# Cosine attention followed by a two-layer GELU network, fused: head pairs on 128 partitions, x kept on chip, second matmul between the next batch's attention steps

## The chip, the cores and the metric

One core of one Trainium2 chip. The metric is the device time of one execution in microseconds (us); below, "span" is the time from the first to the last instruction in the trace, which for the kernel before is 21 us shorter than the measured time. PE is the engine for matmuls; DVE, ACT and POOL are the vector, scalar and GpSimd engines; SP issues transfers. Every figure is of fast runs (within 1.5% of the kernel's fastest).

## The reference, cut to what matters

```python
# q, k, v: (8, 12, 448, 64) float32, tau = 0.1
q_n = q / (norm(q) + 1e-6);  k_n = k / (norm(k) + 1e-6)
attn = softmax(q_n @ k_n.T / tau) @ v                 # per batch and head
x = attn.transpose(0, 2, 1, 3).reshape(8 * 448, 768)  # tokens x d_model
h = x @ w_in                                          # 768 -> 2048
out = gelu_exact(h) @ w_out                           # 2048 -> 768
```

## The kernel before

All 96 heads come first, one by one; then the two matrix products, in blocks of 512 tokens. `x` goes through a bf16 tensor in device memory between the halves.

```python
for b in range(B):
    for h in range(H):
        # ... DMA q, k, v; v to bf16 on POOL with a column of ones ...
        nc.scalar.activation(sq, qk, AF.Square)
        nc.vector.tensor_reduce(nq, sq, mybir.AxisListType.X, ALU.add)
        nc.vector.reciprocal(rn, nq)
        nc.scalar.sqrt(inq, rn)                       # another table than exp
        nc.gpsimd.tensor_tensor(qkb, qk, inq.to_broadcast([CS, NT, 2, D]), ALU.mult)
        # ... 4 transposes on PE, 2 copies on DVE ...
        for c in range(NT):
            nc.tensor.matmul(st, lhsT=qknT[:, 1, c, :], rhs=qknT[:, 0, :, :], start=True, stop=True)
            nc.scalar.activation(pt, st, AF.Exp, scale=float(inv_tau))
            nc.tensor.matmul(acc, lhsT=v1[:, c, :], rhs=pt, start=(c == 0), stop=(c == NT - 1))
        nc.vector.reciprocal(rec, acc[D:D + 1, :])    # 448 values on one partition
        nc.gpsimd.partition_broadcast(rb_, rec)
        nc.vector.tensor_tensor(oT, acc[0:D, :], rb_, ALU.mult)
        nc.sync.dma_start(out=xT[h * D:(h + 1) * D, b * S:(b + 1) * S], in_=oT)
# ... weights loaded and cast on DVE ...
for rb in range(NRB):                                 # 7 blocks of 512 tokens
    # ... load x; first product and gelu; second product, copy, store ...
```

Of the kernel before, what the change touches and what calls it, by code (L numbers as in the profile page):

```python
# [8 lines left out]
F32 = mybir.dt.float32  # L9
BF16 = mybir.dt.bfloat16  # L10
AF = mybir.ActivationFunctionType
ALU = mybir.AluOpType


@with_exitstack
def kernel(
    ctx: ExitStack,
    tc: tile.TileContext,
    q: bass.AP,
    k: bass.AP,  # L20
    v: bass.AP,
    tau: float,
    moe_w_in: bass.AP,
    moe_w_out: bass.AP,
    out: bass.AP,
):
    nc = tc.nc
    B, H, S, D = q.shape
    NT = 4
    CS = S // NT  # L30
    d_model = H * D
    n_tok = B * S
    d_ff = moe_w_in.shape[1]
    inv_tau = 1.0 / float(tau)

    xT = nc.dram_tensor("xT_bridge", (d_model, n_tok), BF16, kind="Internal").ap()

    consts = ctx.enter_context(tc.tile_pool(name="consts", bufs=1))
    ident = consts.tile([CS, CS], BF16)
    make_identity(nc, ident)  # L40

    qkp = ctx.enter_context(tc.tile_pool(name="qkp", bufs=3))
    vp = ctx.enter_context(tc.tile_pool(name="vp", bufs=2))
    hdp = ctx.enter_context(tc.tile_pool(name="hdp", bufs=2))
    stp = ctx.enter_context(tc.tile_pool(name="stp", bufs=3))
    attn_ps = ExitStack()
    ps = attn_ps.enter_context(tc.tile_pool(name="ps", bufs=2, space=bass.MemoryType.PSUM))
    ps2 = attn_ps.enter_context(tc.tile_pool(name="ps2", bufs=3, space=bass.MemoryType.PSUM))

    for b in range(B):  # L50
        for h in range(H):
            qk = qkp.tile([CS, NT, 2, D], F32, tag="qk")
            nc.sync.dma_start(out=qk[:, :, 0, :],
                              in_=q[b, h].rearrange("(c p) d -> p c d", c=NT))
            nc.sync.dma_start(out=qk[:, :, 1, :],
                              in_=k[b, h].rearrange("(c p) d -> p c d", c=NT))
            vf = qkp.tile([CS, NT, D], F32, tag="vf")
            nc.sync.dma_start(out=vf, in_=v[b, h].rearrange("(c p) d -> p c d", c=NT))
            v1 = vp.tile([CS, NT, D + 1], BF16, tag="v1")
            nc.vector.memset(v1[:, :, D], 1.0)  # L60
            nc.gpsimd.tensor_copy(v1[:, :, :D], vf)  # L61

            sq = qkp.tile([CS, NT, 2, D], F32, tag="sq")
            nc.scalar.activation(sq, qk, AF.Square)  # L64
            nq = qkp.tile([CS, NT, 2], F32, tag="nq")
            nc.vector.tensor_reduce(nq, sq, mybir.AxisListType.X, ALU.add)  # L66
            rn = qkp.tile([CS, NT, 2], F32, tag="rn")
            nc.vector.reciprocal(rn, nq)  # L68
            inq = qkp.tile([CS, NT, 2], F32, tag="inq")
            nc.scalar.sqrt(inq, rn)  # L70
            qkb = qkp.tile([CS, NT, 2, D], BF16, tag="qkb")
            nc.gpsimd.tensor_tensor(qkb, qk,  # L72
                                    inq.to_broadcast([CS, NT, 2, D]), ALU.mult)

            tp = ps.tile([2 * D, NT, CS], BF16, tag="tp")
            for c in range(NT):
                nc.tensor.transpose(tp[:, c, :], qkb[:, c, :, :], ident)  # L77
            qknT = hdp.tile([D, 2, NT, CS], BF16, tag="qknT")
            nc.vector.tensor_copy(qknT[:, 0, :, :], tp[0:D, :, :])  # L79
            nc.vector.tensor_copy(qknT[:, 1, :, :], tp[D:2 * D, :, :])  # L80

            acc = ps2.tile([D + 1, S], F32, tag="acc")
            for c in range(NT):
                st = ps2.tile([CS, S], F32, tag="st")
                nc.tensor.matmul(st, lhsT=qknT[:, 1, c, :],  # L85
                                 rhs=qknT[:, 0, :, :], start=True, stop=True)
                pt = stp.tile([CS, S], BF16, tag="pt")
                nc.scalar.activation(pt, st, AF.Exp, scale=float(inv_tau))  # L88
                nc.tensor.matmul(acc, lhsT=v1[:, c, :], rhs=pt,  # L89
                                 start=(c == 0), stop=(c == NT - 1))  # L90
            rec = stp.tile([1, S], F32, tag="rec")
            nc.vector.reciprocal(rec, acc[D:D + 1, :])  # L92
            rb_ = stp.tile([D, S], F32, tag="rb")
            nc.gpsimd.partition_broadcast(rb_, rec)
            oT = stp.tile([D, S], BF16, tag="oT")
            nc.vector.tensor_tensor(oT, acc[0:D, :], rb_, ALU.mult)  # L96
            nc.sync.dma_start(out=xT[h * D:(h + 1) * D, b * S:(b + 1) * S], in_=oT)

    attn_ps.close()

    KD = d_model // 128
    KF = d_ff // 128
    RB = 512
    NRB = n_tok // RB

    wpool = ctx.enter_context(tc.tile_pool(name="wpool", bufs=1))
    wtmp = ctx.enter_context(tc.tile_pool(name="wtmp", bufs=2))
    wi = wpool.tile([128, KD, d_ff], BF16)
    wo = wpool.tile([128, KF, d_model], BF16)
    for kd in range(KD):  # L110
        t = wtmp.tile([128, d_ff], F32, tag="wt1")
        nc.sync.dma_start(out=t, in_=moe_w_in[kd * 128:(kd + 1) * 128, :])
        nc.vector.tensor_copy(wi[:, kd, :], t)
    for kf in range(KF):
        t = wtmp.tile([128, d_model], F32, tag="wt2")
        nc.sync.dma_start(out=t, in_=moe_w_out[kf * 128:(kf + 1) * 128, :])
        nc.vector.tensor_copy(wo[:, kf, :], t)

    xpool = ctx.enter_context(tc.tile_pool(name="xpool", bufs=2))
    gpool = ctx.enter_context(tc.tile_pool(name="gpool", bufs=2))  # L120
    opool = ctx.enter_context(tc.tile_pool(name="opool", bufs=3))
    psm = ctx.enter_context(tc.tile_pool(name="psm", bufs=4, space=bass.MemoryType.PSUM))
    pso = ctx.enter_context(tc.tile_pool(name="pso", bufs=4, space=bass.MemoryType.PSUM))

    NSPLIT = 2
    NSZ = [512, 256]
    NOFF = [0, 512]

    for rb in range(NRB):
        r0 = rb * RB  # L130
        xTb = xpool.tile([128, KD, RB], BF16, tag="xTb")
        for kd in range(KD):
            nc.sync.dma_start(out=xTb[:, kd, :], in_=xT[kd * 128:(kd + 1) * 128, r0:r0 + RB])
        gT = gpool.tile([128, KF, RB], BF16, tag="gT")
        for m in range(KF):
            hp = psm.tile([128, RB], F32, tag="hp")
            for kd in range(KD):
                nc.tensor.matmul(hp, lhsT=wi[:, kd, m * 128:(m + 1) * 128],  # L138
                                 rhs=xTb[:, kd, :],
                                 start=(kd == 0), stop=(kd == KD - 1))  # L140
            nc.scalar.activation(gT[:, m, :], hp, AF.Gelu)  # L141
        for rs in range(RB // 128):
            for ni in range(NSPLIT):
                nsz = NSZ[ni]
                op = pso.tile([128, 512], F32, tag="op")
                for kf in range(KF):
                    nc.tensor.matmul(op[:, :nsz],  # L147
                                     lhsT=gT[:, kf, rs * 128:(rs + 1) * 128],
                                     rhs=wo[:, kf, NOFF[ni]:NOFF[ni] + nsz],
                                     start=(kf == 0), stop=(kf == KF - 1))  # L150
                ot = opool.tile([128, 512], F32, tag="ot")
                nc.vector.tensor_copy(ot[:, :nsz], op[:, :nsz])  # L152
                nc.sync.dma_start(
                    out=out[r0 + rs * 128:r0 + (rs + 1) * 128, NOFF[ni]:NOFF[ni] + nsz],
                    in_=ot[:, :nsz])


# [1 line left out]
_INS = ['q', 'k', 'v', 'tau', 'moe_w_in', 'moe_w_out']  # L159
_OUTS = [((3584, 768), 'float32')]  # L160
#: Inputs that are plain numbers.
_NUMBERS = {'tau': 0.10000000149011612}


# [26 lines left out]
```

## Time and profile before

| | before |
|---|---|
| time, median | 1788 us |
| span of the profiled run | 1767 us |
| attention (96 heads) | 0 to 1471 us |
| two matrix products | 1471 to 1767 us |

The prediction below shows the slices, the chain, the stretches and one head of this profile. Two rows of the page's groups are added here (line, engine, operation, output and input with sizes, count | busy us, mean ns | idle time of the engine before them and what ended it):

```profile
L92 DVE RECIPROCAL rec<-acc 1x448 f32<-1x448 f32 x96 | 283.3, 2952 | 463.2 <-PE acc L89 463.2
L88 ACT ACT_TABLE_LOAD x93 | 119.3, 1283 | 472.1 <-PE st L85 472.1
```

They are to be read together: the reciprocal is DVE's largest item, and DVE stood idle for 463 us before it. An engine that is both busy and waiting like this is a link of a serial chain.

### The profile page before, as it was taken

How to read it: one execution, taken by the hardware profiler on the slowest of the kernel's cores; microseconds unless marked ns; L12 is line 12 of the kernel's file. 1: busy time of each engine (PE TensorE's matmuls, PEld its weight loads, DVE VectorE, ACT ScalarE, POOL GpSimd, SP SyncE). 2: the span in 40 equal slices, each digit the busy share in tenths (PEclk: the TensorE clock that was granted, in tenths of full speed). 3: DMA queues.
4: the chain of work that ended last, by engine and by line, in shares of the span. 5: the costliest groups of instructions: out<-in, count | busy, mean ns of one | idle time of the engine just before them, and what ended most of it. 6: DMA issues, size and time to landing. Idle time of an engine off the chain costs nothing.

```text
span 1767.2 us, 9510 instructions
## 1 busy us (share of the span) xinstructions
PE 700.8 (40%) x2692; PEld 292.8 (17%) x2720; DVE 540.4 (31%) x750; ACT 566.1 (32%) x876; POOL 205.7 (12%) x294
## 2 busy tenths in 40 slices
PE   3222222222222222222222222222222227999999
PEld 1000000000000000000000000000000003555554
DVE  5533332333332333332333333323333331111111
ACT  4333333333333333333333333333333322222222
POOL 1111111111111111111111111111111110000000
PEclk9999999999999999999999999999999999999999
DMA  6511111111111111111111011111111100111111
GB/s 206 164 23 27 27 32 28 34 30 29 30 29 31 28 25 25 27 27 25 27 28 28 22 28 27 26 26 27 28 25 25 27 9 30 57 61 58 60 41 41
DMA packets 158645, 68.27 MB, mean 39 GB/s; under 512 B 137088, under 2 KB 152192, under 8 KB 157824
## 3 DMA queue, kind: packets, MB, share of 16 engines
q1 hardware_dynamic: 158592, 67.67, 14.5%
q8 instruction: 21, 0.34, 0.1%
q14 instruction: 32, 0.26, 0.0%
HBM read 51.12 MB, written 16.52 MB: 38 GB/s over the span
## 4 chain that ended last, share of the span: by engine, by line
PE 39%; issue 29%; DVE 13%; ACT 9%; POOL 6%; DMA 3%; ACTq 0%; POOLq 0%; SPq 0%
PE st L85 10%; PE acc L89 10%; PE hp L138 8%; PE op L147 8%; POOL qkb L72 5%; ACT L70 5%; DVE oT L96 3%; PE tp L77 3%; ACT pt L88 3%; DVE nq L66 3%; DVE qknT L80 2%; DVE qknT L79 2%; DVE rec L92 2%; DMA xTb<-xT_bridge 1%; DMA xT_bridge<-oT 1%
## 5 line engine op out<-in xcount | busy, mean ns | idle before, releaser
L92 DVE RECIPROCAL rec<-acc 1x448 f32<-1x448 f32 x96 | 283.3, 2952 | 463.2 <-PE acc L89 463.2
L77 PE MATMUL tp<-ident,qkb 112*128 112x112 bf16 x384 | 53.2, 294 | 856.8 <-POOL qkb L72 856.8
L88 ACT ACT_TABLE_LOAD x93 | 119.3, 1283 | 472.1 <-PE st L85 472.1
L70 ACT ACT_TABLE_LOAD x93 | 119.3, 1283 | 420.8 <-DVE rn L68 420.7
L85 PE MATMUL st<-qknT 64*112 64x448 bf16 x384 | 190.7, 597 | 85.8 <-DVE qknT L80 84.5
L89 PE MATMUL acc<-pt,v 112*65 112x448 bf16 x384 | 179.3, 565 | 114.5 <-ACT pt L88 114.5
L88 ACT ACTIVATE pt<-st 112x448 bf16<-112x448 f32 x384 | 188.0, 543 | 65.4 <-PE st L85 64.4
L77 PEld LDWEIGHTS <-qkb 112*128 112x128 bf16 x384 | 30.5, 130 | 929.6 <-POOL qkb L72 929.6
L79 DVE COPY qknT<-tp 64x448 bf16<-64x448 bf16 x96 | 36.7, 383 | 469.5 <-PE tp L77 469.5
L72 POOL TENSOR_TENSOR qkb<-qk,inq 112x512 bf16<-112x512 f32 x96 | 99.5, 1037 | 661.5 <-issue 559.5
L138 PE MATMUL hp<-xTb,wi 128*128 128x512 bf16 x658 | 147.5, 383 | 5.5 <-DVE oT L96 4.6
L147 PE MATMUL op<-wo,gT 128*128 128x512 bf16 (+1 forms) x882 | 146.0, 325 | 0.7
L141 ACT ACTIVATE gT<-hp 128x512 bf16<-128x512 f32 x112 | 66.9, 597 | 201.9 <-PE hp L138 201.9
L152 DVE COPY ot<-op 128x512 f32<-128x512 f32 (+1 forms) x56 | 31.3, 558 | 262.3 <-PE op L147 262.3
L85 PEld LDWEIGHTS <-qknT 64*112 64x112 bf16 x384 | 60.9, 187 | 277.1 <-issue 168.4
L147 PEld LDWEIGHTS <-gT 128*128 128x128 bf16 x896 | 87.7, 98 | 59.4
L138 PEld LDWEIGHTS <-wi 128*128 128x128 bf16 x672 | 66.2, 99 | 85.2 <-DVE oT L96 5.8
L89 PEld LDWEIGHTS <-v 112*65 112x65 bf16 x384 | 47.6, 149 | 119.7 <-issue 119.7
L66 DVE TENSOR_REDUCE nq<-sq 112x8 f32<-112x512 f32 x96 | 64.3, 670 | 4.7 <-ACT sq L64 4.7
L64 ACT ACTIVATE sq<-qk 112x512 f32<-112x512 f32 x96 | 59.6, 622 | 0.3 <-DMA qk<-in_k_dram 0.2
L61 POOL CAST v<-vf 112x256 bf16<-112x256 f32 x96 | 48.2, 504 | 5.7 <-issue 5.7
L80 DVE COPY qknT<-tp 64x448 bf16<-64x448 bf16 x96 | 37.7, 393 | 1.3
(205 smaller groups left out, 195.0 us busy)
## 6 DMA issues: line engine op xcount, KB each, us to landing
qk<-in_q_dram SPq DMA_DIRECT2D x96, 112.0 KB, 2.2
qk<-in_k_dram SPq DMA_DIRECT2D x96, 112.0 KB, 2.5
vf<-in_v_dram SPq DMA_DIRECT2D x96, 112.0 KB, 2.1
out_dram<-ot SPq DMA_DIRECT2D x28, 256.0 KB, 2.0
t<-in_moe_w_in_dram SPq DMA_DIRECT2D x6, 1024.0 KB, 5.6
t<-in_moe_w_out_dram SPq DMA_DIRECT2D x16, 384.0 KB, 3.7
xT_bridge<-oT SPq DMA_DIRECT2D x96, 56.0 KB, 1.9
xTb<-xT_bridge SPq DMA_DIRECT2D x42, 128.0 KB, 2.3
```

Source lines behind the costliest of these rows:

```text
L66: nc.vector.tensor_reduce(nq, sq, mybir.AxisListType.X, ALU.add)
L70: nc.scalar.sqrt(inq, rn)
L72: nc.gpsimd.tensor_tensor(qkb, qk, inq.to_broadcast([CS, NT, 2, D]), ALU.mult)
L77: nc.tensor.transpose(tp[:, c, :], qkb[:, c, :, :], ident)
L79: nc.vector.tensor_copy(qknT[:, 0, :, :], tp[0:D, :, :])
L80: nc.vector.tensor_copy(qknT[:, 1, :, :], tp[D:2 * D, :, :])
L85: nc.tensor.matmul(st, lhsT=qknT[:, 1, c, :], rhs=qknT[:, 0, :, :], start=True, stop=True)
L88: nc.scalar.activation(pt, st, AF.Exp, scale=float(inv_tau))
L89: nc.tensor.matmul(acc, lhsT=v1[:, c, :], rhs=pt, start=(c == 0), stop=(c == NT - 1))
L92: nc.vector.reciprocal(rec, acc[D:D + 1, :])
L138: nc.tensor.matmul(hp, lhsT=wi[:, kd, m * 128:(m + 1) * 128], rhs=xTb[:, kd, :], start=(kd == 0), stop=(kd == KD - 1))
L147: nc.tensor.matmul(op[:, :nsz], lhsT=gT[:, kf, rs * 128:(rs + 1) * 128], rhs=wo[:, kf, NOFF[ni]:NOFF[ni] + nsz], start=(kf == 0), stop=(kf ...
```

## The change

The intent: work on two heads at a time, so that 128 partitions are used; lay the score and value matmuls out so that the two heads occupy different halves of PE's array; replace the one-partition reciprocal by ACT's exp(-ln(sum)) on 128 partitions, with the sums made by a matmul against ones; make the norms without ACT's square root (a power on POOL); keep `x` on chip; prepare pairs ahead in a fixed program order; and run the second product of a batch in small pieces ("fillers") between the attention steps of the next batch. Each engine is given its instructions in the order of emission. The diff, cut to its core:

```diff
+    def prep_square(g):                                   # pair g
+        nc.gpsimd.tensor_tensor(sq, qk_t[g], qk_t[g], ALU.mult)
+        nc.vector.tensor_reduce(nq, sq, mybir.AxisListType.X, ALU.add)
+    def prep_scale(g):
+        nc.gpsimd.tensor_tensor(sr, nq, half, ALU.pow)
+        nc.vector.tensor_scalar(se, sr, 1e-6, None, ALU.add)
+        nc.vector.reciprocal(rn, se)
+        # two nc.gpsimd.tensor_tensor(qkb, t, rn, ALU.mult)
+    def transposes(g):
+        # 8 nc.tensor.transpose into one bank, then
+        nc.vector.tensor_copy(qkT, tp)
+    def scores(g, c):                                     # two heads: rows 0:64 and 64:128
+        for h in range(2):
+            nc.tensor.matmul(st[:, h, :S], lhsT=qkT[rows, 1, c, :], rhs=qkT[rows, 0, :, :], ...)
+        nc.scalar.activation(pt, st[:, :, :S], AF.Exp, scale=inv_tau)
+    def values(g, part):                                  # part 0: v, part 1: ones
+        for c in range(NC):
+            for h in range(2):
+                nc.tensor.matmul(dst[h * D:(h + 1) * D, :S], ...)
+    def normalise(g):
+        nc.scalar.activation(ln, sm[:, :S], AF.Ln)
+        nc.scalar.activation(rs, ln, AF.Exp, scale=-1.0)
+        nc.vector.tensor_tensor(x_t[b][:, p, :], o[:, :S], rs, ALU.mult)
...
+        for i in range(HP):                               # attention(b, fill)
+                scores(g, 0); run(u)
+                scores(g, 1); run(u)
+                values(g - 1, 0)
+                scores(g, 2); run(u)
+                values(g - 1, 1)
+                scores(g, 3)
+                normalise(g - 1)
+                upkeep(g)          # loads, prep_square(g + 4), prep_scale(g + 3)
+                run(u)
+                transposes(g + 1)
+                run(...)
...
+    for n in range(1, 4):
+        upto("sq", n, prep_square)
+        upto("sc", n - 1, prep_scale)
+    for kd in range(KD): load_wi(kd)
+    for i in range(4): load_wo(i)
+    upto("sc", 3, prep_scale)
+    transposes(0)
...
+        for m in range(KF):        # first product and gelu of batch b
+            ...
+            if m == KF - 3 and b + 1 < B:
+                transposes((b + 1) * HP)
+        fill += second_pieces(sb, t)
```

## The prediction

> **What bounds the kernel now.** I read four views of the profile, in this order: the page's slices, the chain of work that ended last, the table of stretches, and the timeline of a single head. The slices come first, because they show that the program has two halves that never meet.
>
> ```profile
> PE   3222222222222222222222222222222227999999
> PEld 1000000000000000000000000000000003555554
> DVE  5533332333332333332333333323333331111111
> ACT  4333333333333333333333333333333322222222
> ...
> PE 39%; issue 29%; DVE 13%; ACT 9%; POOL 6%; DMA 3%; ACTq 0%; POOLq 0%; SPq 0%
> ```
>
> For 33 of 40 slices (the attention of 96 heads) no engine is half busy. For the last seven (the two matrix products) PE is full. The last line, the chain by engine, says the same: no engine owns the path, and the time passes from hand to hand. The table of stretches (start:end, length, then busy time and count for PE, weight loads, DVE, ACT, POOL) sets the sizes:
>
> ```profile
> 100.00:700.00 600.00, 166.06 (x468) 56.46 (x468) 197.89 (x269) 203.25 (x310) 82.68 (x117) 1.00 0.12 29
> 1480.00:1767.00 287.00, 282.71 (x1511) 150.28 (x1536) 31.26 (x56) 64.51 (x108) 0.00 (x0) 1.00 0.16 53
> ```
>
> Attention ends at 1471 us, so a head costs 1471 / 96 = 15.3 us; the products take 296 us. One head in the timeline (start, duration, engine, line, operation; in brackets the idle time before it and who ended it):
>
> ```profile
> 698.70 2.95 DVE L92 RECIPROCAL rec<-acc 1x448 f32<-1x448 f32 x1 [5.02 <-PE acc L89]
> 701.69 0.62 DVE L96 TENSOR_TENSOR oT<-acc,rb__2506 64x448 bf16<-64x448 f32 x1
> 702.24 0.67 DVE L66 TENSOR_REDUCE nq<-sq 112x8 f32<-112x512 f32 x1
> 703.22 1.28 ACT L70 ACT_TABLE_LOAD   x1 [4.66 <-DVE rn L68]
> 704.52 0.21 ACT L70 ACTIVATE inq<-rn 112x8 f32<-112x8 f32 x1
> 706.62 1.03 POOL L72 TENSOR_TENSOR qkb<-qk,inq 112x512 bf16<-112x512 f32 x1 [7.09 <-issue]
> 707.71 0.55 PE L77 MATMUL tp<-ident,qkb 112*128 112x112 bf16 x4 [9.05 <-POOL qkb L72]
> 709.15 1.36 PE L85 MATMUL st<-qknT 64*112 64x448 bf16 x3 [0.88 <-DVE qknT L80]
> 709.84 1.28 ACT L88 ACT_TABLE_LOAD   x1 [5.12 <-PE st L85]
> 711.14 1.41 ACT L88 ACTIVATE pt<-st 112x448 bf16<-112x448 f32 x3
> 714.11 2.95 DVE L92 RECIPROCAL rec<-acc 1x448 f32<-1x448 f32 x1 [5.02 <-PE acc L89]
> ```
>
> The reader is to see one long chain per head, with nearly no overlap with the next head: a reciprocal on one partition (2.95), the normalising multiply, the norms of the *next* head queued behind it, a table load for the square root, the square root, the scaling on POOL, transposes, copies, scores, a second table load for the exponential, then the values; 15.4 us after the first reciprocal the next one starts. The kernel is bound by dependence and order, not by an engine.
>
> The same row shows that PE is also slow here: three score matmuls of 448 columns last 1.36 us in all with 0.6 for one, so they start 0.38 apart, 1.2 columns per ns. In the products, at full flow:
>
> ```profile
> 1475.70 18.01 PEld L138 LDWEIGHTS <-wi 128*128 128x128 bf16 x84 [0.22 <-issue]
> ```
>
> 84 steps in 18.01 us are 0.214 us per 512 columns, 2.4 columns per ns. The granted clock reads 1.00 in both stretches and does not show this.
>
> [...]
>
> **The change part by part.**
>
> Removed: the one-partition reciprocal (96 x 2.95 = 283 us, all on the chain), the broadcast on POOL, both table loads per head (186 x 1.283 = 239 us), the square on ACT, the bridge through memory, and the float-to-bf16 copies of v and weights. The order is now fixed so that preparation runs some four pairs ahead; the 15.3 us chain should leave the path altogether, and the question is which engine takes its place. I add each engine for one *pair* of heads (48 of them).
>
> ACT: an exponential of 448 columns takes 543 ns and the gelu of 512 columns 597, so 54 / 64 = 0.84 ns a column and 165 ns fixed. Four exponentials of 896 columns: 4 x 0.92 = 3.7; logarithm and its exponential 2 x 0.54 = 1.1. Sum 4.8 us. In all 48 x 4.8 + 128 gelus x 0.54 + 16 loads x 1.28 = 320 us.
>
> DVE: reduce over 1024 (2 x 0.67 = 1.3), two small operations (0.3), one copy of 896 bf16 columns (0.75), one multiply (0.62): 3.0; with 56 output copies of 0.56 about 175 us. Not the bound.
>
> POOL: scaling of 512 columns takes 1.04, so square of 1024 about 2.05, scaling 2 x 1.04 = 2.1, [...] a wait of about 0.6 for DVE between power and scaling, and the power on 16 columns, for which I leave 1.0 without evidence. Sum 6.7 us.
>
> PE, warm, at 0.42 ns a column: 448 columns 0.188, 384 columns 0.161. Per pair 8 score matmuls = 1.50 and 16 value and sum matmuls = 3.0, both laid out for two tiles of the array at a time. [...] Eight transposes at 0.085 (four take 0.55 with 0.294 for the last): 0.7. The mode changes ten times in a pair (filler, scores, filler, scores, filler, values, scores, filler, sums, scores, transposes). [...] Sum 4.8 us. Filler of 12 or 18 matmuls in a pair adds 1.9 or 2.9: 6.7 or 7.7 us, above ACT's 4.8 and at or above POOL's 6.7. So PE becomes the bound.
>
> The whole span on PE, in us:
> - Batch 0 up to the end of its attention: paced by POOL, which issues six v and ten weight transfers among the first pairs. [...] square and next pair 5.8; [...] third pair 3.7; three pairs at 6.7; last pair through 5: about 60. The 6.3 MB of the first weight, asked for at 21 us, arrive at 0.17 MB/us (the second slice of the page moved 164 GB/s) near 58.
> - First product: 768 x 0.188 = 144.
> - Second product: 896 x 0.161 = 144, all but the last 128 matmuls between attention steps.
> - Attention of seven batches: 42 x 4.8 = 202.
> - Turns of the two shared accumulator banks: where a transpose takes the other bank while an output is summed, the next output wants the bank just filled and waits for its copy, 0.56 (between 425 for 256 columns and 692 for 512) plus a hand-over, 0.65. I count four in a batch of 96 fillers and five in one of 128: 7 x 4.5 x 0.65 = 20. One more for the transposes inside the first product: 7 x 0.9 = 6.
> - Batch starts: exponential table and first exponential before the third score can go, 7 x 2 = 14; end of batch 0, 2.
> - Last copy and store: 3.
>
> Sum 60 + 144 + 144 + 202 + 26 + 16 + 3 = 595. Time exceeds span by 1788.2 - 1767.2 = 21. That gives 616; I say 620.
>
> **The rivals.**
> 1. *Packed matmuls do not overlap.* Then 42 x (4.51 - 2.82) = 71 is added: about 690. For it: the loads of 112 and 65 columns already read 187 and 149 ns each, close to the 188 of a warm matmul, and may not hide when two run together. [...]
> 2. *POOL becomes the bound.* A power of 4 us makes its pair 9.7 against PE's 7.2 on average; and DVE, which executes in order, stands behind the wait for POOL, so copies and then PE stop too: 42 x 2.5 = 105 and 10 in batch 0, about 730. For it: nothing in the trace bounds that operation. Against: it is 16 columns.
> 3. *Perfect packing and free mode changes.* A pair costs 2.26 + 0.7 = 3.0: 42 x 1.8 = 76 less, about 540; with 12 fillers PE would come to 4.9 and share the bound with ACT.
> 4. *ACT reloads tables* between logarithm and exponential: 2.6 more, 7.4 us a pair, at PE's level; perhaps 25 more. Against: both in one set, loaded by hand.
> 5. *The chain survives.* If the next batch still waited for a serial chain, gains would halve, near 1000. Against: four pairs of lead in the order.
>
> **Range and chances.** The middle is the sum. The lower end, 550, is rival 3 with some waits left; the upper, 700, is rival 1 with a little of 2. Even rival 5 leaves the kernel much faster: faster 0.985, same 0.01, slower 0.005.
>
> **What would show it.** In the new profile: PE at nine tenths from about slice 5 on; score matmuls of two heads starting a few ns apart (packing) or 0.19 apart (rival 1); about 16 or 17 table loads; POOL under 400 us busy and its power near 1 us; [...] about 60 us before the first gelu. The prediction is wrong if PE idles more than a fifth of the span after 60 us, if POOL's busy share is near 90%, or if the chain that ended last names DVE or POOL for more than a quarter.

The sum came to 595 us of span (60 + 144 + 144 + 202 + 26 + 16 + 3) and 616 of time; it said 620. The marked cuts took out what no trace or run of this case shows. Terms that are cut, or that have lost their reason, are still in these sums: 1.0 us on POOL for the issue of one transfer (in its 6.7 us a pair, and in batch 0, where 60 was 15 to the first scaled pair, 6 of it for six v transfers, then 5.8, 10 for ten weight transfers, 3.7, three times 6.7, and 5); packed matmuls at 1.6 times the speed (0.94 + 1.88 in place of 1.50 + 3.0); and 0.13 us for each of ten mode changes, that is, changes of the array's division between matmuls (1.3). PE's pair was 0.94 + 1.88 + 0.7 + 1.3 = 4.8. The kernel after shows 0.74 us for the issue of a v transfer, and 0.56 and 0.75 for those of the two weights. The wait of 0.6 us on POOL was my estimate (the kernel after shows 0.57 in its first pairs). That logarithm and exponential share a table was not shown by the kernel before; the kernel after ran its 48 pairs with 16 table loads.

## The result, and the profile after

| | before | after |
|---|---|---|
| time, median | 1788.9 us | 740.5 us (735.9 to 745.5) |
| span of the profiled run | 1767 us | 734.4 us |
| first product of batch 0 starts | | 97.3 us |
| PE busy | 40% | 74% |

The ratio is 0.4141 (95% interval 0.4117 to 0.4166). Here and below a ratio is the mean time of one kernel's fast runs over that of the kernel before in the same rounds, so it is not quite the ratio of the medians. The changed kernel is 2.4 times as fast, and still 120 us slower than the predicted 620 and outside the range. Its four runs fall in two groups, near 736 and 745 us; the profiled run is of the first. What separates them is not known, so small differences are read below from profiled runs.

From the page after: two rows of the slices, the start of the chain, and two groups.

```profile
PE   0056588577968698757986879776987679867997
...
PEclk9999899879997999878998899887998889988999
...
PE 66%; DVE 12%; ACT 10%; issue 5%; POOL 4%; DMA 2%; SPq 0%; POOLq 0%
...
L136 PE MATMUL st<-qkT 64*112 64x448 bf16 x384 | 88.8, 471 | 140.9 <-DVE qkT L127 128.1
...
L107 POOL TENSOR_TENSOR sr<-nq,half 112x16 f32<-112x16 f32 x48 | 140.2, 2920 | 0.0
```

PE now owns most of the chain, as predicted, but it is not full: its digits fall to 5 to 7 again and again. The granted clock falls with it. (The traces have no clock record before 1475.6 us in the kernel before and 80.8 us in the changed one, and the views count that time as full rate. But scores start 0.38 us apart there in the kernel before (84 matmuls of the same width later take 16.05 us in the changed one, 0.19 each), and eight transposes take 0.93 us in the changed one, against 0.56 later; so the mean clocks given here are too high.) The score group says whom PE waited for: 128 us for DVE's copy `qkT`. The last row is the unknown that the prediction left at 1.0 us: the power on 16 columns takes 2.92 us.

The waits of the kernel after (who waited for whom: total us, times, longest):

```profile
POOL qkb L115 <- DVE rn L111: 282.3, 47, 15.3
...
DVE x L160 <- ACT rs L159: 243.8, 48, 9.6
...
PE st L136 <- DVE qkT L127: 128.1, 31, 20.5
```

POOL, the engine with the long power, waits for DVE; DVE waits for ACT; PE waits for DVE. The timeline shows why. One pair's end in the kernel after (start, duration, engine, line, operation; idle time in brackets):

```profile
239.68 0.40 PE L136 MATMUL st<-qkT 64*112 64x448 bf16 x2
...
240.12 0.92 ACT L139 ACTIVATE pt<-st 112x896 bf16<-112x896 f32 x1 [1.04 <-PE st L136]
240.67 0.56 PE L125 MATMUL tp<-ident,qkb 112*128 112x112 bf16 x8
240.94 0.54 ACT L157 ACTIVATE ln<-sm 128x448 f32<-128x448 f32 x1
...
241.50 0.58 ACT L159 ACTIVATE rs<-ln 128x448 f32<-128x448 f32 x1
242.11 0.62 DVE L160 TENSOR_TENSOR x<-o,rs 128x448 bf16<-128x448 f32 x1 [2.97 <-ACT rs L159]
242.65 1.21 DVE L101 TENSOR_REDUCE nq<-sq 112x16 f32<-112x1024 f32 x1
...
244.15 0.56 DVE L127 COPY qkT<-tp 128x896 bf16<-128x896 bf16 x1
...
244.76 0.62 PE L136 MATMUL st<-qkT 64*112 64x448 bf16 x2 [3.21 <-DVE qkT L127]
245.32 1.46 PE L175 MATMUL op<-wo,g 128*128 128x384 bf16 x4
```

The transposes are done at 241.23. DVE is idle then, and could copy them at once. But next in DVE's queue stands the normalising multiply `x` of the *previous* pair, which waits for ACT: the last exponential, the logarithm, the second exponential. Behind it stand a reduce of 1.21 us and two small operations that belong to a pair three or four places ahead. Only then, at 244.15, comes the copy, and PE has stood still for 3.21 us. The last row shows the second cost: four fillers take 1.46 us instead of 0.82 (as at 240.01), because PE has dropped to half rate (granted clock 0.50 from 244.7 to 247.2).

Two stretches carry the miss. Batch 0 ended at 97.3 instead of 62 us (60, and 2 for its end; +35). The seven periods between the starts of first products average (690.5 - 97.3) / 7 = 84.7 us; the prediction's terms give 18.0 + 28.8 + 17.7 + 3.7 + 2 = 70.2 (+14.5 each, +102). Together this is 137 of the 139 us by which the span exceeds the predicted 595.

### The profile page after: what moved, and what is told of

It reads as the page before. It is cut to its first block, busy times and chain, and to the rows that moved or that the text cites. A ratio compares the mean times of both kernels' runs of the same rounds, so it can differ in the third digit from the quotient of the medians.

```text
span 734.4 us, 7898 instructions
## 1 busy us (share of the span) xinstructions
PE 545.8 (74%) x3200; PEld 249.3 (34%) x3200; DVE 156.3 (21%) x298; ACT 312.9 (43%) x432; POOL 367.2 (50%) x256
## 4 chain that ended last, share of the span: by engine, by line
PE 66%; DVE 12%; ACT 10%; issue 5%; POOL 4%; DMA 2%; SPq 0%; POOLq 0%
PE op L175 21%; PE hp L281 20%; PE st L136 10%; PE o L149 8%; PE sm L149 6%; DVE nq L101 4%; DVE x L160 3%; ACT rs L159 3%; ACT ln L157 3%; DVE qkT L127 3%; POOL sr L107 2%; ACT pt L139 1%; ACT L287 1%; DMA wi<-in_moe_w_in_dram 1%; ACT g L283 1%
## 5 line engine op out<-in xcount | busy, mean ns | idle before, releaser
L139 ACT ACTIVATE pt<-st 112x896 bf16<-112x896 f32 x192 | 173.4, 917 | 282.5 <-PE st L136 282.3
L115 POOL TENSOR_TENSOR qkb<-qk,rn 112x512 bf16<-112x512 f32 x96 | 98.1, 1043 | 284.5 <-DVE rn L111 282.3
L175 PE MATMUL op<-wo,g 128*128 128x384 bf16 x896 | 206.4, 365 | 0.2
L136 PE MATMUL st<-qkT 64*112 64x448 bf16 x384 | 88.8, 471 | 140.9 <-DVE qkT L127 128.1
L281 PE MATMUL hp<-x,wi 128*128 128x448 bf16 x768 | 148.1, 353 | 2.3 <-ACT g L283 1.7
L107 POOL TENSOR_TENSOR sr<-nq,half 112x16 f32<-112x16 f32 x48 | 140.2, 2920 | 0.0
L283 ACT ACTIVATE g<-hp 128x448 bf16<-128x448 f32 x128 | 69.7, 544 | 90.5 <-PE hp L281 90.5
L175 PEld LDWEIGHTS <-g 128*128 128x128 bf16 x896 | 78.3, 104 | 86.2 <-issue 56.9
L99 POOL TENSOR_TENSOR sq<-qk 112x1024 f32<-112x1024 f32 x48 | 91.4, 1905 | 2.2 <-DMA qk<-in_k_dram 1.1
L149 PE MATMUL o<-pt,v 112*64 112x448 bf16 x384 | 61.2, 454 | 13.5 <-DVE x L160 13.5
```

Of the source, the lines that this page charges most:

```text
L99: nc.gpsimd.tensor_tensor(sq, qk_t[g], qk_t[g], ALU.mult)
L107: nc.gpsimd.tensor_tensor(sr, nq, half, ALU.pow)
L115: nc.gpsimd.tensor_tensor(qkb[:, i].rearrange("p c h d -> p h c d"), t[:, i], rn[:, i].to_broadcast([CS, 2, NC, D]), ALU.mult)
L136: nc.tensor.matmul(st[:, h, :S], lhsT=qkT[rows, 1, c, :], rhs=qkT[rows, 0, :, :], start=True, stop=True)
L139: nc.scalar.activation(pt, st[:, :, :S], AF.Exp, scale=inv_tau)
L149: nc.tensor.matmul(dst[h * D:(h + 1) * D, :S], lhsT=v_t[g][:, h, c, :] if part == 0 else ones, rhs=pt_t[g, c][:, h, :], start=(c == 0), st ...
```

## The experiments

Theory ORDER: the loss comes from the order of DVE's queue, in which the copy that PE needs stands behind work that waits for ACT. Theory POOL: the power of 2.92 us makes POOL the pacemaker (rival 2 of the prediction, whose 730 us lies close to the measured time). Twelve kernels were run, in three groups; those of a group shared a chip.

**1. A cheap operation in place of the power** (outputs wrong)

```diff
-        nc.gpsimd.tensor_tensor(sr, nq, half, ALU.pow)
+        nc.gpsimd.tensor_tensor(sr, nq, half, ALU.add)
```

> One operator changed: the power on POOL (2.92 us, 48 of them) becomes an addition (about 0.1 to 0.2 us); the outputs are wrong on purpose. Theory ORDER: in each pair PE waits for the DVE copy of the transposes, which stands in DVE's queue behind the normalising multiply (waits for ACT's logarithm and exponential) and a reduce; POOL is ahead and waits 2.5 to 5 us for DVE, so the power is off the path except at the start, where the third pair's power (2.9 us) stands before the first copy: 732 to 742 us. Theory POOL: POOL's queue paces the pairs, so 2.75 us less in each of 47 pairs, about 130 us: 600 to 640 us.

Measured: 736.8 us, ratio 0.4129 (0.4118 to 0.4140). The addition took 0.22 us in place of 2.92, POOL's busy time fell from 367 to 236 us and the time hardly moved. POOL waited for DVE 409 us instead of 282: what it gained it spent waiting. Between the profiled runs (736.2 and 728.1 us) there are 8 us, all before the first product (97.3 and 88.6); the period after it is 84.7 and 84.8. POOL does not pace the pairs of this kernel. The number of rival 2 was right by accident.

**2. The copy first in DVE's queue**

```diff
-            if i > 0:
-                normalise(g - 1)
-            upkeep(g)
             run(u)
             if i < HP - 1:
                 transposes(g + 1)
+            if i > 0:
+                normalise(g - 1)
+            upkeep(g)
             run(per_slot - ...)
```

The compiled programs were compared row by row: PE's, ACT's and POOL's rows are the same in the same order; only DVE's order differs (and, following it, the place of some transfers in SP's queue).

> Only the order of DVE's instructions is changed: the copy of the next pair's transposes (and an output copy) stands ahead of the normalising multiply and the reduce; PE's, ACT's and POOL's instructions and their order are the same as in the changed kernel. Theory ORDER: the 3.2 us wait of PE in each of about 40 pairs goes, and with it the half clock behind it; POOL's own 8.2 us a pair is then the next floor: 570 to 610 us. Theory POOL: no gain beyond 2%, 725 to 740 us.

Measured: 619.4 us, ratio 0.3472 (0.3460 to 0.3484), correct. The order of one queue is worth 121 us. In the profiled runs, 114 us apart, the seven periods carry 100 (84.7 to 70.4 us each). The time is a little above the expected 570 to 610; the third run shows why. The same place of a pair in this run:

```profile
196.53 0.40 PE L136 MATMUL st<-qkT 64*112 64x448 bf16 x2 [0.39 <-DVE qkT L127]
...
202.53 0.56 PE L125 MATMUL tp<-ident,qkb 112*128 112x112 bf16 x8
...
203.12 0.62 DVE L127 COPY qkT<-tp 128x896 bf16<-128x896 bf16 x1 [1.80 <-PE tp L125]
...
203.80 0.40 PE L136 MATMUL st<-qkT 64*112 64x448 bf16 x2 [0.39 <-DVE qkT L127]
203.97 0.62 DVE L160 TENSOR_TENSOR x<-o,rs 128x448 bf16<-128x448 f32 x1 [0.22 <-ACT rs L159]
```

The copy starts as soon as the transposes end, PE waits 0.39 us instead of 3.21, and a pair with 18 fillers takes 203.80 - 196.53 = 7.27 us.

**3. Both edits** (outputs wrong)

> Both edits of the first two runs (wrong outputs on purpose). Theory ORDER with POOL as the next floor: 30 to 60 us less than the run with the copy first alone, so 530 to 570. If POOL was never a floor: within 2% of the run with the copy first alone.

Measured: 581.0 us, ratio 0.3255 (0.3246 to 0.3264): the gain is as expected, the time above the expected 570. With the copy first, the same cheap operation that gave nothing in the periods before gives 38 us. In the profiled runs, 15 us of it lie before the first product (83.4 to 68.2). Most of the rest lies around the first products: the time between ACT's two table loads there (the gelu table, then the exponential table) is 22.5 to 27.9 us in the second run, here 20.0 to 21.7, 24 us over seven batches. The longest of them, in the second run:

```profile
157.26 0.17 DVE L109 TENSOR_SCALAR se<-sr 112x16 f32<-112x16 f32 x1 [1.65 <-POOL sr L107]
...
158.12 1.01 DVE L179 COPY ot<-op 128x384 f32<-128x384 f32 x2
...
158.72 18.94 PE L281 MATMUL hp<-x,wi 128*128 128x448 bf16 x84 [3.12 <-DVE ot L179]
```

At the batch's end DVE's next item waits for POOL's power, and behind it stand the output copies that free the accumulator bank for the first product. PE stands still for 3.12 us and then runs at half rate for a while (granted clock 0.53 from 158.7 to 165; 84 matmuls in 18.94 us, in the third run 16.05). It is the same fault of order with POOL in ACT's place. So POOL was a second floor, hidden under the first.

**4. The inverse root on ACT, order as in the changed kernel** (right outputs)

```diff
-        nc.gpsimd.tensor_tensor(sr, nq, half, ALU.pow)
-        nc.vector.tensor_scalar(se, sr, 1e-6, None, ALU.add)
-        nc.vector.reciprocal(rn, se)
+        nc.scalar.activation(ls, nq, AF.Ln)
+        nc.scalar.activation(rn, ls, AF.Exp, scale=-0.5)
```

(Leaving out the 1e-6 kept the result within the check.)

> A right kernel without the power on POOL: the inverse root is made by ACT as exponential of -0.5 times the logarithm (16 columns each, about 0.2 us each), and DVE's addition and reciprocal go as well. The order of the copy stays as in the changed kernel. Theory ORDER: 0.45 us of DVE work leaves the wait in each pair and 0.4 us is added behind on ACT, and the first copy no longer waits for the third power: 705 to 735 us. Theory POOL: 600 to 640 us.

Measured: 714.6 us, ratio 0.4010 (0.3993 to 0.4026), correct. In the profiled runs (719.7 against 736.2) the first product of batch 0 started at 83.1 instead of 97.3 us, and the period fell only from 84.7 to 84.4: nearly all of the gain is in batch 0. Within ORDER's range, far from POOL's.

**5. The copy first, and the inverse root on ACT**

> The copy first on DVE, and the inverse root on ACT instead of POOL; right outputs. Theory ORDER, with POOL as second floor: the same as the run with copy first and the cheap wrong power (581), give or take 2%: 570 to 592; the transposes inside the first product no longer wait for POOL (about 6 us in each of seven batches in the run with the copy first alone). If the 38 us between those two runs came from something else than POOL's power: near 619.

Measured: 577.5 us, ratio 0.3228 (0.3212 to 0.3244), correct. A correct kernel confirms the third run.

**6. Also the first pair's copy ahead of the weight transfers**

```diff
+    transposes(0)
     for kd in range(KD):
         load_wi(kd)
     ...
     upto("sc", 3, prep_scale)
-    transposes(0)
```

The start of the changed kernel has the same fault in the order of the queue. The first pair's transposes, the third pair's power, the copy and the first scores there; below them the first scores of the fifth run:

```profile
16.04 0.56 PE L125 MATMUL tp<-ident,qkb 112*128 112x112 bf16 x4 [0.44 <-POOL qkb L115]
...
33.16 2.93 POOL L107 TENSOR_TENSOR sr<-nq,half 112x16 f32<-112x16 f32 x1
...
36.49 0.56 DVE L127 COPY qkT<-tp 128x896 bf16<-128x896 bf16 x1
...
37.11 0.99 PE L136 MATMUL st<-qkT 64*112 64x448 bf16 x4 [20.51 <-DVE qkT L127]
```

```profile
16.52 1.00 PE L134 MATMUL st<-qkT 64*112 64x448 bf16 x4 [3.08 <-DVE qkT L125]
```

> As the run before, and the first pair's transposes and their copy are issued ahead of the weight transfers and of the third pair's preparation. Theory: the start is held by the same kind of order on DVE (first scores at 37 us although the transposes ended at 17), so up to 18 us less: 555 to 575. Rival: the first weight's arrival sets the first product's start anyway, then no gain beyond 3 us against the run before.

Measured: 575.9 us, ratio 0.3226 (0.3215 to 0.3237): no gain against the fifth run (0.3228), and just outside the expected range. The edit had nothing left to remove: the wait up to 37 us was the changed kernel's, and in the fifth run the first scores already start at 16.5 us (here 16.1), because without the power the copy is no longer held. What held batch 0 in both runs is another wait. In the sixth run ACT stood still from 20 to 32 us, because POOL was busy or blocked with ten weight transfers from 16 to 26 us and the next pairs were not ready. The first product moved from 69.1 to 62.6 us, but not by the edit: the last pairs of batch 0 took 6.7 us in the fifth run, where the granted clock reads 7 and 6 tenths in the slices from 43 to 72 us, and 5.2 in the sixth, where it reads 9 from 43 to 57 us, and the eighth run, whose start is the same as the sixth's, began it at 66.2. The result fits the rival's number (no gain beyond 3 us); its reason, the weight's arrival, is not what PE waited for.

**7. The second product in one piece, order as in the changed kernel**

```diff
-            fill += second_pieces(sb, t)
+            for f in second_pieces(sb, t):
+                f()
```

> The changed kernel with one part undone: the second product runs in one piece after the first product of each batch, and not between the next batch's attention steps. Theory ORDER: a pair without filler still takes about 10 us (batch 0's pace), with filler 12, so the filler hides only about a third to a half of itself: 800 to 860 us. If the interleaving gave nothing: 730 to 750. If it hid all of the second product: 740 + 124 = 864 or more.

Measured: 781.1 us, ratio 0.4372, correct; below the expected range. A pair without filler took 9.2 to 10.4 us (7.8 to 9.0 in the last batch), as expected (batch 0 of the changed kernel: mostly 10.05), and a pair with filler 9.7 to 12.6; but the first pair of a batch, whose first scores are done by then, takes about 7 with filler, which the expectation left out. Interleaving 768 x 0.161 = 124 us of matmuls saves 41 us, a third.

**8. The two heads' value matmuls one after the other**

```diff
-        for c in range(NC):
-            for h in range(2):
+        for h in range(2):
+            for c in range(NC):
```

> As the run with all three edits, but the sixteen value and sum matmuls of a pair run head by head, so that neighbours use the same half of the array's columns. If the packing is real and PE is the bound by then: 8 x 0.188 = 1.5 us more in each of 48 pairs, 72 us, so 60 to 75 more than the run before. If the two halves never ran at the same time: within 2% of it.

Measured: 576.4 us, ratio 0.3227: the same as the sixth run, and by the expectation this would have meant that nothing ever ran at the same time. The trace says otherwise. Eight value matmuls and the scores behind them, and a stretch of 0.04 us at the start (length, then busy time and count for PE and DVE, clock, DMA share, GB/s):

```profile
181.66 0.96 PE L147 MATMUL o<-pt,v 112*64 112x448 bf16 x8
...
182.55 0.40 PE L134 MATMUL st<-qkT 64*112 64x448 bf16 x2
```

```profile
181.64:181.68 0.04, 0.02 (x2) 0.00 (x0) 1.00 0.74 179
```

Eight matmuls of 448 columns are through in 0.89 us, where one by one they would need 8 x 0.188 = 1.50, and two start in the same 0.04 us although in the compiled program the first four belong to one head and the next four to the other. The records do not name the head of each matmul, so this is read from the count, the times and the compiled order. The edit did not do what it was meant to do; a run that does was needed.

**9. The two heads kept apart by other matmuls**

```diff
-                values(g - 1, 0)
+                values(g - 1, 0, (0,))
             scores(g, 2)
+                values(g - 1, 0, (1,))
             run(u)
-                values(g - 1, 1)
+                values(g - 1, 1, (0,))
             scores(g, 3)
+                values(g - 1, 1, (1,))
```

> As the run with all three edits, but the two heads' value (and sum) matmuls are kept apart by the score matmuls, which use another division of the array, so that they cannot run together; in the run with heads apart the trace showed both heads starting together although four matmuls of one head stood ahead of the other's. If packing is real and PE is the bound: 8 x 0.188 = 1.5 us and two more mode changes of 0.13, 1.8 us in 40 pairs, up to 72 us, less where PE waited anyway: 50 to 72 more than 576. If not: about 10 more.

Measured: 629.6 us, ratio 0.3530 (0.3514 to 0.3546), 54 us more than the sixth run. Four matmuls of one head now take as long as eight did:

```profile
200.46 0.94 PE L147 MATMUL o<-pt,v 112*64 112x448 bf16 x4
201.33 0.40 PE L134 MATMUL st<-qkT 64*112 64x448 bf16 x2
```

The packing is real and complete (two heads in the time of one). The 54 us are a little more than its worth for the value and sum matmuls: a pair takes 1.74 us longer (8.36 against 6.62), of which 8 x 0.188 = 1.50 is the lost packing; the rest, 0.24, goes with the two further changes of the array's division that the edit adds.

**10. The second product in one piece, with all three edits**

> The second product in one piece again, now with the three edits. In batch 0 of the edited kernel a pair without filler takes 5.2 us, ACT's own sum; with 18 fillers it takes 7.3. So the interleaving hides about 0.8 us of filler in each of 42 pairs and some of the batch ends: 610 to 630. If it hid all the filler: 576 + 124 = 700. If nothing: 576.

Measured: 608.5 and 617.4 us in the two fast runs, ratio 0.3435 (0.3402 to 0.3468), correct; the other two (621.7 and 632.0) count as slow. By the ratios interleaving is worth 37 us here, against 41 in the seventh run. The clock averaged 0.929 in the profiled run against 0.990 in the sixth; pairs took 4.4 to 5.2 us, or 6.7 where PE ran at half rate (eight sum matmuls in 1.71 us, where they took 0.95 in the pair before).

**11. The weight transfers spread over the first pairs**

```diff
-    for kd in range(KD):
+    for kd in range(2):
         load_wi(kd)
-    for i in range(4):
-        load_wo(i)
...
             upkeep(g)
+            if b == 0 and i < 2:
+                load_wi(2 + 2 * i)
+                load_wi(3 + 2 * i)
+            if b == 0 and i > 1:
+                load_wo(i - 2)
```

> As the run with all three edits, but ten weight transfers are not issued in one block on POOL's queue (which held the third pair's preparation from 16 to 26 us there): two at first, four in the first two pairs, four in the next four pairs. If POOL's block sets the start: the first product begins near 52 instead of 62.6 us, and the time falls by 6 to 10: 564 to 571. If the weights' arrival sets it: within 1% of 576.

Measured: 568.9 us (566.5 to 570.2), ratio 0.3184 (0.3169 to 0.3199), correct: the fastest kernel, 23% less time than the changed one. The time is in the expected range, but the first product started at 60.5 and not near 52 us: the block on POOL was gone, but batch 0's last pairs ran at 6.7 us instead of 5.2, largely at half rate (eight sum matmuls in 1.71 us at 39.5; the granted clock reads 8 and 7 tenths in the slices from 28 to 57 us). The medians are 7 us apart, the profiled runs 3.6, of which 2.1 lie before the first product; where the rest comes from stays open.

**12. Ten more matmuls where PE waits, order as in the changed kernel**

```diff
     def scores(g, c):
         ...
+        if c == 0 and g % HP > 0:
+            for _ in range(10):
+                nc.tensor.matmul(st[:, 0, :S], lhsT=qkT_t[g - 1][:, 1, 0, :],
+                                 rhs=qkT_t[g - 1][:, 0, :, :], start=True, stop=True)
```

> The changed kernel as it was, with ten more full-array matmuls (1.9 us at full clock) placed where PE waits for DVE's copy at the start of each pair but a batch's first; their output is overwritten. If part of the loss is that PE falls to half clock after the 3.2 us wait: less time with more work, 680 to 715. If the clock costs nothing because the chain over ACT and DVE paces the pair: 738 to 760.

Measured: 709.0 us, ratio 0.3967 (0.3946 to 0.3987), correct: 31 us *less* time with 400 more matmuls.

```profile
222.69 0.40 PE L140 MATMUL st<-qkT 64*112 64x448 bf16 x2 [1.32 <-DVE qkT L127]
223.02 0.82 PE L179 MATMUL op<-wo,g 128*128 128x384 bf16 x4
```

PE's idle stretch is 1.32 us instead of 3.21, the four fillers behind it take 0.82 instead of 1.46, and the mean clock of the profiled run rose from 0.904 to 0.969. So part of the loss in the changed kernel is the half rate that follows a wait such as that of 3.21 us (clock 0.50); after the wait of 1.32 us it does not show. The chain over ACT and DVE is the cause, the clock an amplifier of it.

## Why the prediction was wrong, point by point

**What bounds the kernel before, and that the chain goes: right in direction.** The table loads fell from 188 to 16, the reciprocal and the bridge are gone, and the time fell by 59%.

**The step that failed** is "the 15.3 us chain should leave the path altogether", and with it "Not the bound" for DVE's 3.0 us a pair. I added up each engine's busy time for a pair and compared the sums; I did not follow the order of DVE's queue, though the diff shows it. DVE was busy for 156 us, no more than the 175 of the sum, and it was still the engine that held PE, because the order in its queue tied PE's next pair to ACT's last step of the previous one. Experiment 2 shows it: moving the copy ahead, with nothing else changed on PE, ACT or POOL, takes 121 us away. Rival 2 did say that DVE executes in order and would stop PE, but named POOL as the engine waited for; experiment 1 refutes that for the pairs of this kernel, and experiment 3 shows it at the batch ends once the copy was moved. Rival 5 asked whether a serial chain would survive and dismissed it with "four pairs of lead in the order": the lead held for the loads and norms, not for the copy.

**Batch 0, predicted 60 us, measured 97.** The first scores could start only at 37 us, behind the third pair's power (same fault, at the start), and then a pair took 10.05 us instead of the 6.7 that I had given POOL. Without the power (experiment 4) the first scores start at 16.0 us, but the second pair's only at 34.0, behind the ten weight transfers on POOL.

**The power, predicted 1.0 us with no evidence, measured 2.92**, more than a multiply of 112 x 1024 (1.91). POOL's pair is 0.74 + 1.91 + 2.92 + 2 x 1.04 = 7.7 us without waits, where I had 6.1 and 0.6 of waiting. In the changed kernel the power cost some 4 us by the medians and 8 by the profiled runs, all in batch 0, and some 40 once the order was mended (experiments 2, 3 and 5).

**PE's attention work, predicted 4.8 us a pair, measured 3.8.** From the starts in the timeline of experiment 2: four score steps of 0.33, two groups of eight value matmuls at 0.88, transposes 0.39: 3.47. Three of the four groups of four fillers take 0.75 up to the packed group that follows, and the one before the transposes 0.66, which adds 3 x 0.09: about 3.8. Packing gave the full factor 2 (experiment 9) and not the 1.6 that I had assumed, and the transposes took 0.39 and not 0.7. The mode changes come to about 1.1 us a pair, near the predicted 1.3: a packed pair of scores takes 0.33 us up to the next filler's start, 0.14 more than one matmul of 448 columns (0.188), and four fillers take 0.75 up to a packed group and 0.66 up to the transposes, which use the whole array as they do, so 0.09 goes with the change before a packed group. So rival 3 was right on perfect packing and wrong on free mode changes. The error, 42 x 1.0 = 42 us, was on the safe side and hid a part of the order's cost: with PE's term mended my sum would have been 595 - 42 = 553, and the miss in span 181 us, not 139.

**The products and the ending: right.** The last first product took 18.2 us (predicted 18.0), the last 128 fillers 20.8 (20.6). ACT's exponential of 896 columns took 917 ns (0.92), and the tables were loaded 16 times. What was not right is the step from span to time: 21 us carried over from the kernel before, 1.8 here (736.2 - 734.4).

**The signs to watch.** The prediction said it would be wrong if PE idled more than a fifth of the span after 60 us: (545.8 - 13.3) us busy in 674 is 79%, just over that line. POOL was 50% busy over the span. The third sign, a chain that names DVE or POOL for more than a quarter, stayed silent: it names DVE for 12% and POOL for 4%. So the shares of that chain did not show that DVE's order held PE; the timeline did. One reading was wrong as well: that no engine is half busy in 33 slices leaves out DVE's digit 5 in the first two.

Open: the share of the half rate in the 121 us (experiment 12 gives 31 us as a lower value, since a wait of 1.3 us remained), where the fastest kernel gained after its first product, and what separates the two groups of runs of the changed kernel.

## What to carry to other kernels

Sums of busy time tell which engine can be the bound, not which one is: for each engine that executes in order, write down its queue and ask of every item what it waits for and who waits for the item behind it. Put what the bound engine needs next ahead of what finishes the previous step. When a fix of one suspected cost gives nothing, try it again after the other one is mended: the power on POOL was worth 4 to 8 us before the copy was moved, and some 40 after.
